# TensorE's instructions kept in source order from the third token group on, and the attention's state products put right behind its output products

## Chip, cores and metric

One Trainium2 chip, one core. The metric is device time in microseconds of one launch, less is better. The kernel before takes 876.1 us (median of three runs, 875.66 to 876.71).

## What is computed

Three layers, one behind the other, on 4 x 768 = 3072 tokens of width 8 x 48 = 384: a gated linear attention with a decaying state, a gated feed-forward layer behind an RMS norm, and a layer of 8 experts of which each token uses one.

```python
def _attn_ref(q, k, v, alpha):
    for t in range(S):
        state = alpha[:, :, t, :, None] * state + np.einsum('bhd,bhe->bhde', k[:, :, t], v[:, :, t])
        y[:, :, t] = np.einsum('bhd,bhde->bhe', q[:, :, t], state)
...
def _moe_ref(x, w_gate, w_val, w_out, rms_g):
    xn = x / np.sqrt(np.mean(x * x, axis=-1, keepdims=True) + 1e-06) * rms_g
    g = xn @ w_gate
    return g * (1.0 / (1.0 + np.exp(-g))) * (xn @ w_val) @ w_out
...
def _moe2_ref(x, w_gate, w_output_gate, w1, w2):
    e_idx = np.argmax(x @ w_gate, axis=1)
    for e in range(E):
        mask = e_idx == e
        h = np.maximum(x[mask] @ w1[e], 0.0)
        out[mask] = gate_w[mask, None] * eom[mask, e, None] * (h @ w2[e])
```

## The kernel before

The tokens are cut into 24 tiles of 128, three tiles to a group, so there are eight groups (`g` 0 to 7). Tiles 0 to 17 take turns among three of the four sequences, tiles 18 to 23 are the fourth sequence. The attention goes chunk by chunk: a chunk is one tile, and its sequential loop is replaced by products inside the tile and a state carried from tile to tile of a sequence.

**Attention, `stages(t)`.** Five stages for a tile, each a short piece of TensorE work and a closure `post` with what other engines do behind it:

- score (`ps_s`, line 416): eight products of q and k, one for each head, even heads on the lower rows of the array and odd heads on the upper ones. Behind it VectorE multiplies by the mask (`P`, line 426), and the state is decayed and copied to `wide` (lines 420, 422).
- transposes of k (`ps_k`, line 436), copied to `kn` by ScalarE.
- output (`ps_y`): four products of q with the state (line 447), sixteen of `P` with v (line 451). Behind it the RMS norm: square and sum on ScalarE, a power on GpSimd, the scaling to `xn` on ScalarE (lines 457 to 460).
- state (`ps_st`, line 472): eight products of k and v, added to the state by VectorE. The last tile of a sequence has neither this nor the transposes of k.
- transposes of `xn` (`ps_x`, line 493), copied to the feed-forward layer's input in a high and a low part, `xh` and `xl`.

Ahead of them `prework(t)` prepares q and k with scans and multiplications on VectorE. From tile 8 on it uses no TensorE.

**Feed-forward layer.** A group makes 36 slots: for each of 12 blocks of 128 hidden columns a gate product (`ps_g`), a value product (`ps_v`) and an output product (`ps_o`). Each slot is nine matmuls of 384 or 400 columns in fp32r, because every operand is split in a high and a low part (`mm3`, line 595, and `m_out`, line 629). VectorE multiplies gate and value (`tt`, line 606) and makes the low part `hl` (line 615); ScalarE makes the gate's activation and the high part `hh` (lines 587, 609). Groups 0 and 1 are cut in two runs each (`runs`), and while they run the weights arrive and are converted on VectorE and ScalarE: `F` or `Fo`, then the high part, then the low part (`wgl`, `wvl`, `wol`, line 531).

**What sets the order.** The loops call `slot` for a slot and `stage` for the next stage when it is due; `NST` (5) is the number of stages a tile counts for. That is the order of the source. The program is then put in order for each engine by a scheduler, which runs the instructions through a model of the engines and lets an engine take a later instruction when an earlier one isn't ready in the model. `tc.keep_in_program_order(ins)` takes that freedom away: instructions marked so keep the order of the source among themselves on their engine. `pace` marks a few on other engines; TensorE's products of the attention and of the feed-forward layer are not marked.

**PSUM.** The attention's tiles share three banks (pool `psA`), the feed-forward layer has five.

After the eight groups come the experts (`e_h`, `e_o`), from about 625 us to the end.

Of the kernel before, what the change touches and what calls it, by code (L numbers as in the profile page):

```python
# [42 lines left out]
    'RB': 9,  # L43
    'LEADG': 6,
    'NAT': 5,
    'PET': 8,
    'NO': 'arkq',
}
# [4 lines left out]
def gla_glu_moe_kernel(  # L53
# [16 lines left out]
    nc = tc.nc  # L70
    P = 128
    B, H, S, D = q.shape
# [3 lines left out]
    NTILE = NT // P  # L76
    KD = DM // P
# [5 lines left out]
    GT = 3  # L83
# [20 lines left out]
    ident = const.tile([P, P], F32, name="ident")  # L104
# [9 lines left out]
    tri_b = const.tile([P, P], BF16, name="tri_b")  # L114
    ones_b = const.tile([P, P], BF16, name="ones_b")
# [86 lines left out]
    vt = {}  # L202
    pre = {}
    xT = {}
    SEATS = CFG['SEATS']
    spread = [True]
    junk = [psM.tile([P, 4, P], F32, tag='o2', name='junk')]
    paced = [CFG['K0']]

# [191 lines left out]
    def stages(t):  # L401
        b, c = place_of[t]
        first, final = c == 0, c == NCH - 1
        en, qT, kT = pre[t]
        Sc = state_of[b % BS]
        S_ = wide[0]
        rs = [slice(64 * hh, 64 * hh + D) for hh in range(2)]
        g, ti = divmod(t, GT)
        Pt = {}

        def score():
            ps = [bank([P, NP, P], "ps_s") for _ in range(2)]
            for p in range(NP):
                for hh in range(2):
                    r = slice(64 * hh, 64 * hh + D)
                    nc.tensor.matmul(ps[hh][:, p, :], lhsT=kT[r, p, :], rhs=qT[r, p, :], start=True, stop=True)  # L416

            def post():
                if not first:
                    nc.vector.tensor_tensor(out=Sc, in0=Sc, in1=en.to_broadcast([P, NP, D]), op=ALU.mult)  # L420
                    for hh in range(2):
                        nc.scalar.activation(S_[rs[hh], :, hh * D:hh * D + D], Sc[rs[hh]], AF.Copy)
                mb = mask.to_broadcast([P, NP, P])
                for hh in range(2):
                    Ph = seat_of(t, f"P{hh}", [P, NP, P])
                    pace(f'Ph{t}', nc.vector.tensor_tensor(out=Ph, in0=ps[hh], in1=mb, op=ALU.mult))
                    Pt[hh] = Ph
            return post
        yield score

        def ktr():
            if final:
                return None
            ps = bank([P, NP, P], "ps_k")
            for p in range(NP):
                nc.tensor.transpose(ps[:, p, :], kT[:, p, :], ident)  # L436
            kn = seat_of(t, "kn", [P, H, 64])
            nc.scalar.activation(kn, ps.rearrange("p a (h d) -> p (a h) d", h=2), AF.Copy)
            Pt["kn"] = kn
            return None  # L440
        yield ktr

        def outp():
            ps = bank([P, DM], "ps_y")
            if not first:
                for p in range(NP):
                    nc.tensor.matmul(ps[:, p * 2 * D:p * 2 * D + 2 * D], lhsT=qT[:, p, :], rhs=S_[:, p, :],  # L447
                                     start=(p == 0), stop=False, skip_group_check=True)
            for h in (0, 2, 4, 6, 1, 3, 5, 7):
                for u in (slice(0, 64), slice(64, P)):  # L450
                    nc.tensor.matmul(ps[u, h * D:h * D + D], lhsT=Pt[h % 2][:, h // 2, u], rhs=vt[t][:, h, :],  # L451
                                     start=first, stop=True, skip_group_check=True)
# [12 lines left out]
        def state():  # L465
            if final:
                return None
            kn = Pt["kn"]
            ps = bank([P, NP, D], "ps_st")
            for p in range(NP):  # L470
                for hh in range(2):
                    nc.tensor.matmul(ps[64 * hh:64 * hh + 64, p, :], lhsT=kn[:, 2 * p + hh, :],  # L472
                                     rhs=vt[t][:, 2 * p + hh, :], start=True, stop=True)

            def post():
                if first:
                    nc.scalar.activation(Sc, ps, AF.Copy)
                else:
                    nc.vector.tensor_tensor(out=Sc, in0=ps, in1=Sc, op=ALU.add)
            return post  # L480
        yield state

        def xtr():
            if t and t + 2 < NTILE:
                load_v(t + 2)
            if ti == 0:
                xT[g] = (act.tile([P, KD, G], F32R, tag="xh", name="xh"),
                         act.tile([P, KD, G], F32R, tag="xl", name="xl"))
            xh, xl = xT[g]
            xn = Pt["xn"]  # L490
            ps = bank([P, KD, P], "ps_x")
            for kc in range(KD):
                nc.tensor.transpose(ps[:, kc, :], xn[:, kc * P:kc * P + P], ident)  # L493
# [84 lines left out]
    obank = {}  # L578
# [12 lines left out]
    def mm3(ps, wh, wl, xh, xl):  # L591
        n = 0
        for kc in range(KD):
            for a_, b_ in ((wh, xh), (wh, xl), (wl, xh)):
                nc.tensor.matmul(ps, lhsT=a_[:, kc, :], rhs=b_[:, kc, :],  # L595
                                 start=(n == 0), stop=(n == 3 * KD - 1))
                n += 1

    def m_val(g, j):
# [21 lines left out]
    def m_out(s, j):  # L621
        g, j0, j1 = runs[s]
        if j == j0:
            obank[s] = [psM.tile([P, WO], F32, tag=f"o{i}", name="ps_o") for i in range(GT)]
        hh, hl, _ = hbuf.pop((g, j))
        for i in range(GT):
            sl = slice(i * P, i * P + P)
            for n, (a_, b_) in enumerate(((hh, "woh"), (hh, "wol"), (hl, "woh"))):
                nc.tensor.matmul(obank[s][i], lhsT=a_[:, sl], rhs=weight(b_, j),  # L629
                                 start=(j == j0 and n == 0), stop=(j == j1 - 1 and n == 2))  # L630

    rows = {}

# [55 lines left out]
    def route_b(g):  # L689
        oh, ohb, ohc, m8, og, se = rt.pop(g)  # L690
        R = rows[g]
        ps = psR[0].tile([P, GT + 1, E], F32, tag=psR[1], name="ps_r")
        nc.tensor.matmul(ps[:, 0:1, :], lhsT=tri_b, rhs=ohb[:, 0:1, :], start=True, stop=True)
        for i in range(1, GT):
            nc.tensor.matmul(ps[:, i, :], lhsT=tri_b, rhs=ohb[:, i, :], start=True, stop=False)
            nc.tensor.matmul(ps[:, i, :], lhsT=ones_b, rhs=ohc[:, i - 1, :], start=False, stop=True)
        nc.tensor.matmul(ps[:, GT, :], lhsT=ones_b, rhs=ohc[:, GT - 1, :], start=True, stop=True)
        bc = [P, GT, E]

        nc.vector.tensor_scalar(out=se, in0=se, scalar1=1e-9, scalar2=2.0, op0=ALU.add, op1=ALU.mult)  # L700
# [83 lines left out]
            m_out(s - 1, runs[s - 1][2] - 1)  # L784
            return lambda: m_evac(s - 1)

    NST = 5
    LOADS = CFG['LOADS']
    for x in LOADS.split():
        if x[0] == "v":  # L790
# [41 lines left out]
    spread[0] = False  # L832
    prep.extend(prework(GT))

    att_stream = (st for t in range(GT, NTILE) for st in stages(t))
    nprep = GT + 1
    AHEAD = CFG['AHEAD']
    done = 0
    GS = GT * NST
# [385 lines left out]
    u = U - 1  # L1225
# [121 lines left out]
```

## Time and profile before

| | us |
|---|---|
| median of three runs | 876.1 |
| the profiled execution | 880.26 |
| its span, first to last instruction | 878.6 |
| TensorE busy with matmuls | 856.1 |
| TensorE's weight loads | 814.5 |
| VectorE busy | 489.3 |
| ScalarE busy | 326.0 |
| chain that ended last: share of TensorE | 85% |

A busy share counts an instruction from start to end, and TensorE's matmuls overlap each other, so that the row of busy time says little of how fast they follow. In the timeline the distance from one start to the next is what counts. There one instruction of an fp32 product shows as two records (x2), so x16 is all eight score products of a tile.

### The profile page before, as it was taken

How to read it: one execution, taken by the hardware profiler on the slowest of the kernel's cores; microseconds unless marked ns; L12 is line 12 of the kernel's file. 1: busy time of each engine (PE TensorE's matmuls, PEld its weight loads, DVE VectorE, ACT ScalarE, POOL GpSimd, SP SyncE). 2: the span in 40 equal slices, each digit the busy share in tenths (PEclk: the TensorE clock that was granted, in tenths of full speed). 3: DMA queues.
4: the chain of work that ended last, by engine and by line, in shares of the span. 5: the costliest groups of instructions: out<-in, count | busy, mean ns of one | idle time of the engine just before them, and what ended most of it. 6: DMA issues, size and time to landing. Idle time of an engine off the chain costs nothing.

```text
span 878.6 us, 15655 instructions
## 1 busy us (share of the span) xinstructions
PE 856.1 (97%) x6042; PEld 814.5 (93%) x6042; DVE 489.3 (56%) x1108; ACT 326.0 (37%) x708; POOL 143.8 (16%) x204
## 2 busy tenths in 40 slices
PE   7999999999999999999999999999999999999994
PEld 6799999899999999999999999999988999999994
DVE  7899987576854656655665552244454443444330
ACT  1655554234333233332322333334234442445431
POOL 2001001001100100010010010013032343344331
PEclk8999999999999999999999999999999999999998
DMA  9855534493311222132231010023056164256510
GB/s 190 181 163 149 175 83 122 117 258 89 104 49 36 78 57 61 43 87 60 59 87 47 13 37 1 1 93 98 1 182 197 60 212 144 65 190 198 178 41 24
DMA packets 121660, 88.46 MB, mean 101 GB/s; under 512 B 58219, under 2 KB 116716, under 8 KB 121584
## 3 DMA queue, kind: packets, MB, share of 16 engines
q1 hardware_dynamic: 117120, 77.97, 33.4%
q0 software_dynamic: 4464, 9.48, 3.1%
q8 instruction: 48, 0.79, 0.4%
q14 instruction: 28, 0.23, 0.1%
HBM read 71.62 MB, written 16.07 MB: 100 GB/s over the span
## 4 chain that ended last, share of the span: by engine, by line
PE 85%; DMA 5%; issue 4%; DVE 2%; POOL 1%; ACT 1%; SPq 1%; POOLq 0%; DVEq 0%; ACTq 0%
PE ps_o L629 18%; PE ps_v L595 18%; PE ps_g L595 18%; PE ps_b L1037 8%; PE ps_h L595 7%; PE ps_s L416 4%; PE ps_y L451 3%; DMA st<-in_moe_w_dram 3%; PE ps_y L447 2%; DMA er<-bucket 1%; PE ps_st L472 1%; PE ps_k L436 1%; PE ps_x L493 1%; POOL out_dram L1053 1%; PE pc L560 1%
## 5 line engine op out<-in xcount | busy, mean ns | idle before, releaser
L606 DVE TENSOR_TENSOR tt<-tt,ps_v 128x384 f32<-128x384 f32 x96 | 52.8, 550 | 140.9 <-PE ps_v L595 136.5
L587 ACT ACTIVATE tt<-ps_g 128x384 f32<-128x384 f32 x96 | 47.0, 490 | 135.4 <-PE ps_g L595 132.3
L609 ACT ACTIVATE hh<-tt 128x384 fp32r<-128x384 f32 x96 | 50.2, 523 | 119.6 <-DVE tt L606 119.2
L615 DVE TENSOR_TENSOR hl<-tt,hh 128x384 fp32r<-128x384 f32 x96 | 54.4, 567 | 28.1 <-ACT hh L609 27.4
L1037 PE MATMUL ps_b<-w2a,h 128*128 128x384 f32 (+2 forms) x336 | 67.4, 339 | 1.1 <-ACT h L1021 1.1
L595 PE MATMUL ps_g<-xh,wgh 128*128 128x384 f32 x192 | 68.1, 355 | 0.0
L595 PE MATMUL ps_v<-xh,wvh 128*128 128x384 f32 x192 | 68.0, 354 | 0.0
L1022 DVE SCALAR_TENSOR_TENSOR h<-ps_h,h 128x256 fp32r<-128x256 f32 (+6 forms) x72 | 38.0, 531 | 52.3 <-ACT h L1021 52.0
L629 PE MATMUL ps_o<-wol,hh 128*128 128x400 f32 x192 | 66.6, 347 | 0.0
L629 PE MATMUL ps_o<-woh,hh 128*128 128x400 f32 x192 | 66.5, 353 | 0.0
L1037 PE MATMUL ps_b<-w2b,h 128*114 128x384 f32 (+3 forms) x336 | 65.0, 338 | 0.2 <-ACT h L1021 0.2
L595 PE MATMUL ps_g<-xh,wgl 128*128 128x384 f32 x192 | 65.1, 339 | 0.0
L595 PE MATMUL ps_v<-xh,wvl 128*128 128x384 f32 x192 | 65.0, 339 | 0.0
L595 PE MATMUL ps_g<-xl,wgh 128*128 128x384 f32 x192 | 64.9, 338 | 0.0
L629 PE MATMUL ps_o<-woh,hl 128*128 128x400 f32 x192 | 64.7, 346 | 0.0
L595 PE MATMUL ps_v<-xl,wvh 128*128 128x384 f32 x192 | 64.7, 337 | 0.0
L1037 PEld LDWEIGHTS ps_b<-w2a,h 128*128 128x128 f32 (+2 forms) x336 | 57.5, 181 | 2.6 <-ACT h L1021 2.0
L1037 PEld LDWEIGHTS ps_b<-w2b,h 128*114 128x114 f32 (+3 forms) x336 | 57.5, 175 | 2.1 <-ACT h L1021 0.6
L595 PE MATMUL ps_h<-x,w1b 128*128 128x456 f32 (+3 forms) x288 | 58.5, 344 | 0.3 <-DVE h L1022 0.2
L1021 ACT ACTIVATE h<-ps_h 128x256 fp32r<-128x256 f32 (+6 forms) x72 | 33.3, 467 | 64.8 <-PE ps_h L595 60.4
L595 PE MATMUL ps_h<-x,w1a 128*128 128x256 f32 (+3 forms) x288 | 53.5, 328 | 0.6 <-DVE h L1022 0.6
L458 POOL TENSOR_SCALAR ss<-ss 128x1 f32<-128x1 f32 x24 | 6.4, 266 | 281.0 <-ACT xn L457 276.1
(284 smaller groups left out, 1994.9 us busy)
## 6 DMA issues: line engine op xcount, KB each, us to landing
st<-in_moe_w_dram SPq DMA_DIRECT2D x64, 384.0 KB, 5.4
bucket<-zero SPq DMA_DIRECT2D x8, 772.0 KB, 6.2
stg<-in_moe_w_gate_dram SPq DMA_DIRECT2D x12, 384.0 KB, 3.9
stg<-in_moe_w_val_dram SPq DMA_DIRECT2D x12, 384.0 KB, 3.7
stg<-in_moe_w_out_dram SPq DMA_DIRECT2D x12, 384.0 KB, 3.0
v<-in_v_dram SPq DMA_DIRECT2D x23, 192.0 KB, 2.8
blk_a<-in_alpha_dram SPq DMA_DIRECT2D x32, 96.0 KB, 2.2
blk_k<-in_k_dram SPq DMA_DIRECT2D x32, 96.0 KB, 2.3
```

The lines of the kernel that those rows point to most:

```text
L416: nc.tensor.matmul(ps[hh][:, p, :], lhsT=kT[r, p, :], rhs=qT[r, p, :], start=True, stop=True)
L447: nc.tensor.matmul(ps[:, p * 2 * D:p * 2 * D + 2 * D], lhsT=qT[:, p, :], rhs=S_[:, p, :], start=(p == 0), stop=False, skip_group_check=True)
L451: nc.tensor.matmul(ps[u, h * D:h * D + D], lhsT=Pt[h % 2][:, h // 2, u], rhs=vt[t][:, h, :], start=first, stop=True, skip_group_check=True)
L587: nc.scalar.activation(tt, ps, AF.Silu)
L595: nc.tensor.matmul(ps, lhsT=a_[:, kc, :], rhs=b_[:, kc, :], start=(n == 0), stop=(n == 3 * KD - 1))
L606: nc.vector.tensor_tensor(out=tt, in0=tt, in1=ps, op=ALU.mult)
L609: nc.scalar.activation(hh, tt, AF.Copy)
L615: nc.vector.tensor_tensor(out=hl, in0=tt, in1=f(hh), op=ALU.subtract)
L629: nc.tensor.matmul(obank[s][i], lhsT=a_[:, sl], rhs=weight(b_, j), start=(j == j0 and n == 0), stop=(j == j1 - 1 and n == 2))
L1021: nc.scalar.activation(hh[:, 0, :], ps, AF.Relu)
L1022: nc.vector.scalar_tensor_tensor(out=hh[:, 1, :], in0=ps, scalar=0.0, in1=f(hh[:, 0, :]), op0=ALU.max, op1=ALU.subtract)
L1037: ins = nc.tensor.matmul(ob2[u][i][0:r], lhsT=hh[:, a_, sl], rhs=we[p][b_][:, j, :], start=(j == 0 and m == 0), stop=(j == KF2 - 1 and m = ...
```

## The change

Two things, both in the order of work; no product is added or left out.

- `seq` marks TensorE's products of the attention, the feed-forward layer and the routing to keep their source order. It is on in groups 2 to 6, off in groups 0 and 1 and in the last.
- `four` joins output and state to one stage, for tiles 3 to 23. `NST` is 4, so a tile's stages come three slots apart instead of 2.4. `XO` makes a stage due one slot earlier in the runs of groups 0 and 1 behind the first.

```diff
+    'XO': 1,
+    'STRICT': 4,
...
+    strict = [False]
+
+    def seq(ins):
+
+        if strict[0]:
+            tc.keep_in_program_order(ins)
...
-                    nc.tensor.matmul(ps[hh][:, p, :], lhsT=kT[r, p, :], rhs=qT[r, p, :], start=True, stop=True)
+                    seq(nc.tensor.matmul(ps[hh][:, p, :], lhsT=kT[r, p, :], rhs=qT[r, p, :], start=True, stop=True))
...
-    NST = 5
+    NST = 4
...
+    def four(t):
+
+        s_, k_, y_, d_, x_ = stages(t)
+
+        def yd():
+            posts = [y_(), d_()]
+
+            def post():
+                for p in posts:
+                    if p:
+                        p()
+            return post
+        return s_, k_, yd, x_
+
+    att_stream = (st for t in range(GT, NTILE) for st in four(t))
...
-        return (n + 1 + N * (s - 2)) * GS >= (k_ + 1) * 2 * N and k_ < GS and (k_ < NST - 1 or s >= CFG['XG'])
+        return (n + 1 + CFG['XO'] + N * (s - 2)) * GS >= (k_ + 1) * 2 * N and k_ < GS and (k_ < NST - 1 or s >= CFG['XG'])
...
+        strict[0] = s >= CFG['STRICT']
...
+        strict[0] = g + 2 >= CFG['STRICT'] and not last
```

The same `seq(...)` stands around the products of `ktr`, `outp`, `state`, `xtr`, `mm3`, `m_out` and `route_b`.

On TensorE in the third group, from the end of one tile (`ps_x`) over the next tile of the attention, before (each line "..." stands for a slot or more of the feed-forward layer, nine matmuls each):

```order
L493 MATMUL ps_x<-ident,xn 128x128 x3
...
L416 MATMUL ps_s<-qT,kT 128x128
...
L416 MATMUL ps_s<-qT,kT 128x128 x7
...
L436 MATMUL ps_k<-ident,kT 128x128 x4
...
L447 MATMUL ps_y<-wide_125,qT 128x96
...
L447 MATMUL ps_y<-wide_125,qT 128x96
...
L447 MATMUL ps_y<-wide_125,qT 128x96 x2
L451 MATMUL ps_y<-v,P_3041 64x48 x8
L451 MATMUL ps_y<-v,P_3043 64x48 x8
...
L472 MATMUL ps_st<-v,kn 64x48 x8
```

And the same tile in the changed kernel:

```order
L502 MATMUL ps_x<-ident,xn 128x128 x3
...
L425 MATMUL ps_s<-qT,kT 128x128 x8
...
L445 MATMUL ps_k<-ident,kT 128x128 x4
...
L456 MATMUL ps_y<-wide_125,qT 128x96 x4
L460 MATMUL ps_y<-v,P_3041 64x48 x8
L460 MATMUL ps_y<-v,P_3043 64x48 x8
L481 MATMUL ps_st<-v,kn 64x48 x8
```

Eight pieces between slots became four, with three slots between any two of them: the score is whole, the output is whole, and the state products follow it.

On VectorE in the first group, where nothing is marked by `seq` but the scheduler's order follows TensorE's, before (`aT`, `qT`, `kT` are the preparation of an attention tile, `stg`, `F`, `Fo` a weight block):

```order
L531 TENSOR_TENSOR wgl_198<-F_654,wgh_197 128x3x128
L420 TENSOR_TENSOR state1_123<-state1_123,en_576 128x192
L315 SCALAR_TENSOR_TENSOR qT_556<-ps_n_571,begin_127 128x512
L340 TENSOR_TENSOR kT_557<-ps_n_656,aT_555 128x512
L515 TENSOR_SCALAR Fo_744<-stg_173 128x384
L531 TENSOR_TENSOR wvl_316<-F_697,wvh_315 128x3x128
L304 MEMSET begin_127 128x3
L606 TENSOR_TENSOR tt_715<-tt_715,ps_v_726 128x384
```

And the same place in the changed kernel:

```order
L429 TENSOR_TENSOR state1_123<-state1_123,en_596 128x192
L540 TENSOR_TENSOR wgl_198<-F_631,wgh_197 128x3x128
L615 TENSOR_TENSOR tt_694<-tt_694,ps_v_711 128x384
L324 SCALAR_TENSOR_TENSOR qT_576<-ps_n_591,begin_127 128x512
L540 TENSOR_TENSOR wvl_316<-F_685,wvh_315 128x3x128
L524 TENSOR_SCALAR Fo_729<-stg_173 128x384
L540 TENSOR_TENSOR wol_517<-Fo_589,woh_516 128x400
```

The multiplication `tt`, which needs the value product from TensorE, now stands ahead of a scan and of a weight block's low part, and the multiplication of `kT` has gone further back.

## Rows read from the trace of the kernel before

**Rows 1.** Span and mean granted TensorE clock of the core.

```profile
core 0: 878.6 us, clock 0.990
```

**Rows 2.** Busy time in two stretches; columns: stretch, sum, PE, PEld, DVE, ACT, POOL, PEclk, DMA.

```profile
40.00:100.00 60.00, 59.42 (x498) 56.70 (x498) 57.21 (x133) 34.94 (x83) 3.51 (x7) 1.00 0.56 158
195.00:555.00 360.00, 360.00 (x2733) 340.99 (x2732) 203.40 (x484) 116.83 (x279) 32.59 (x63) 1.00 0.22 56
```

**Rows 3.** TensorE's timeline: nine matmuls of one slot, first and ninth; columns: start, us.

```profile
249.05 0.34 PE L595 MATMUL ps_v<-xh,wvh 128*128 128x384 f32 x1
...
250.44 0.34 PE L595 MATMUL ps_v<-xh,wvl 128*128 128x384 f32 x1
```

**Rows 4.** TensorE's timeline: the score products of one tile, cut in one and seven.

```profile
242.18 0.34 PE L595 MATMUL ps_g<-xh,wgl 128*128 128x384 f32 x1
242.45 0.48 PE L416 MATMUL ps_s<-qT,kT 48*128 48x128 f32 x2
242.86 0.44 PE L595 MATMUL ps_v<-xh,wvh 128*128 128x384 f32 x1
243.14 0.34 PE L595 MATMUL ps_v<-xl,wvh 128*128 128x384 f32 x1
...
246.30 1.16 PE L416 MATMUL ps_s<-qT,kT 48*128 48x128 f32 x14
247.38 0.45 PE L595 MATMUL ps_g<-xh,wgh 128*128 128x384 f32 x1
```

**Rows 5.** TensorE's timeline: a tile whose eight score products stand together.

```profile
222.94 1.16 PE L416 MATMUL ps_s<-qT,kT 48*128 48x128 f32 x16
224.04 0.18 PE L693 MATMUL ps_r<-ohb,tri_b 128*128 128x8 bf16 x1
```

**Rows 6.** TensorE's timeline: output and state products of one tile, cut.

```profile
252.51 0.34 PE L629 MATMUL ps_o<-woh,hl 128*128 128x400 f32 x1
252.69 0.36 PE L447 MATMUL ps_y<-wide,qT 128*128 128x96 f32 x2
...
253.09 0.34 PE L595 MATMUL ps_g<-xl,wghe 128*128 128x384 f32 x1
...
256.28 0.58 PE L447 MATMUL ps_y<-wide,qT 128*128 128x96 f32 x4
256.79 1.14 PE L451 MATMUL ps_y<-v,P 128*64 128x48 f32 x32
257.86 0.45 PE L629 MATMUL ps_o<-woh,hh 128*128 128x400 f32 x1
...
261.00 0.34 PE L595 MATMUL ps_g<-xh,wgle 128*128 128x384 f32 x1
261.27 0.67 PE L472 MATMUL ps_st<-v,kn 128*64 128x48 f32 x16
261.87 0.44 PE L595 MATMUL ps_v<-xh,wvhe 128*128 128x384 f32 x1
262.15 0.34 PE L595 MATMUL ps_v<-xl,wvhe 128*128 128x384 f32 x1
```

**Rows 7.** TensorE's timeline: output and state products that stand together in an early tile.

```profile
145.54 1.14 PE L451 MATMUL ps_y<-v,P 128*64 128x48 f32 x32
146.50 0.64 PE L472 MATMUL ps_st<-v,kn 128*64 128x48 f32 x16
147.07 0.44 PE L595 MATMUL ps_v<-xh,wvhe 128*128 128x384 f32 x1
```

**Rows 8.** VectorE's and ScalarE's timelines: mask and norm of the same tile.

```profile
247.28 1.29 DVE L426 TENSOR_TENSOR P<-ps_s,mask 128x512 f32<-128x512 f32 x2 [0.77 <-PE ps_s L416]
...
259.59 0.58 ACT L460 ACTIVATE xn<-ps_y,ss 128x384 f32<-128x384 f32 x1 [0.94 <-POOL ss L459]
```

**Rows 9.** VectorE's costliest groups; columns: busy us, mean ns, idle before.

```profile
L315 DVE TENSOR_TENSOR_SCAN aT<-aT,begin 128x512 f32<-128x512 f32 x19 | 23.1, 1217 | 0.1
L340 DVE TENSOR_TENSOR kT<-ps_n,aT 128x512 f32<-128x512 f32 x3 | 2.0, 670 | 0.0
```

More of the change, by code (lines that the diff above doesn't have):

```diff
@@ L435, in ktr @@
             for p in range(NP):
-                nc.tensor.transpose(ps[:, p, :], kT[:, p, :], ident)
+                seq(nc.tensor.transpose(ps[:, p, :], kT[:, p, :], ident))
             kn = seat_of(t, "kn", [P, H, 64])
@@ L446, in outp @@
                 for p in range(NP):
-                    nc.tensor.matmul(ps[:, p * 2 * D:p * 2 * D + 2 * D], lhsT=qT[:, p, :], rhs=S_[:, p, :],
-                                     start=(p == 0), stop=False, skip_group_check=True)
+                    seq(nc.tensor.matmul(ps[:, p * 2 * D:p * 2 * D + 2 * D], lhsT=qT[:, p, :], rhs=S_[:, p, :],
+                                     start=(p == 0), stop=False, skip_group_check=True))
             for h in (0, 2, 4, 6, 1, 3, 5, 7):
                 for u in (slice(0, 64), slice(64, P)):
-                    nc.tensor.matmul(ps[u, h * D:h * D + D], lhsT=Pt[h % 2][:, h // 2, u], rhs=vt[t][:, h, :],
-                                     start=first, stop=True, skip_group_check=True)
+                    seq(nc.tensor.matmul(ps[u, h * D:h * D + D], lhsT=Pt[h % 2][:, h // 2, u], rhs=vt[t][:, h, :],
+                                     start=first, stop=True, skip_group_check=True))
             def post():
@@ L471, in state @@
                 for hh in range(2):
-                    nc.tensor.matmul(ps[64 * hh:64 * hh + 64, p, :], lhsT=kn[:, 2 * p + hh, :],
-                                     rhs=vt[t][:, 2 * p + hh, :], start=True, stop=True)
+                    seq(nc.tensor.matmul(ps[64 * hh:64 * hh + 64, p, :], lhsT=kn[:, 2 * p + hh, :],
+                                     rhs=vt[t][:, 2 * p + hh, :], start=True, stop=True))
             def post():
@@ L492, in xtr @@
             for kc in range(KD):
-                nc.tensor.transpose(ps[:, kc, :], xn[:, kc * P:kc * P + P], ident)
+                seq(nc.tensor.transpose(ps[:, kc, :], xn[:, kc * P:kc * P + P], ident))
             sl = slice(ti * P, ti * P + P)
@@ L594, in mm3 @@
             for a_, b_ in ((wh, xh), (wh, xl), (wl, xh)):
-                nc.tensor.matmul(ps, lhsT=a_[:, kc, :], rhs=b_[:, kc, :],
-                                 start=(n == 0), stop=(n == 3 * KD - 1))
+                seq(nc.tensor.matmul(ps, lhsT=a_[:, kc, :], rhs=b_[:, kc, :],
+                                 start=(n == 0), stop=(n == 3 * KD - 1)))
                 n += 1
@@ L628, in m_out @@
             for n, (a_, b_) in enumerate(((hh, "woh"), (hh, "wol"), (hl, "woh"))):
-                nc.tensor.matmul(obank[s][i], lhsT=a_[:, sl], rhs=weight(b_, j),
-                                 start=(j == j0 and n == 0), stop=(j == j1 - 1 and n == 2))
+                seq(nc.tensor.matmul(obank[s][i], lhsT=a_[:, sl], rhs=weight(b_, j),
+                                 start=(j == j0 and n == 0), stop=(j == j1 - 1 and n == 2)))
     rows = {}
@@ L692, in route_b @@
         ps = psR[0].tile([P, GT + 1, E], F32, tag=psR[1], name="ps_r")
-        nc.tensor.matmul(ps[:, 0:1, :], lhsT=tri_b, rhs=ohb[:, 0:1, :], start=True, stop=True)
+        seq(nc.tensor.matmul(ps[:, 0:1, :], lhsT=tri_b, rhs=ohb[:, 0:1, :], start=True, stop=True))
         for i in range(1, GT):
-            nc.tensor.matmul(ps[:, i, :], lhsT=tri_b, rhs=ohb[:, i, :], start=True, stop=False)
-            nc.tensor.matmul(ps[:, i, :], lhsT=ones_b, rhs=ohc[:, i - 1, :], start=False, stop=True)
-        nc.tensor.matmul(ps[:, GT, :], lhsT=ones_b, rhs=ohc[:, GT - 1, :], start=True, stop=True)
+            seq(nc.tensor.matmul(ps[:, i, :], lhsT=tri_b, rhs=ohb[:, i, :], start=True, stop=False))
+            seq(nc.tensor.matmul(ps[:, i, :], lhsT=ones_b, rhs=ohc[:, i - 1, :], start=False, stop=True))
+        seq(nc.tensor.matmul(ps[:, GT, :], lhsT=ones_b, rhs=ohc[:, GT - 1, :], start=True, stop=True))
         bc = [P, GT, E]
@@ L833, in gla_glu_moe_kernel @@
     prep.extend(prework(GT))
-    att_stream = (st for t in range(GT, NTILE) for st in stages(t))
+    def four(t):
[9 more added lines that the diff above has]
+    att_stream = (st for t in range(GT, NTILE) for st in four(t))
     nprep = GT + 1
```

## Prediction

> **What bounds the kernel now.** I read the clock first, then the busy time by stretch, then TensorE's timeline, start by start. The granted clock is 0.990 over the span [rows 1] and 1.00 in both stretches that matter here [rows 2], so no term below hangs on it. From 195 to 555 us, where the change pins TensorE's order, TensorE is busy 360.00 of 360 us while VectorE has 203.40 and ScalarE 116.83 [rows 2]: TensorE sets the pace, and nothing else is near its limit. From 40 to 100 us it is otherwise: VectorE has 57.21 of 60 us [rows 2], since it converts weights there, and whatever TensorE saves there is worth little.
>
> That TensorE is "busy" all the time says nothing of how well. Matmuls overlap, so the distance between starts is the price. Inside a slot it is (250.44 - 249.05) / 8 = 0.174 us [rows 3]. At a piece of the attention it is more: a piece costs its own products and an edge on either side. With the single score product of rows 4 the two neighbours are 243.14 - 242.18 = 0.96 us apart where two strides would be 0.35, so this one product costs 0.61 us. Its seven sisters need, from their start to the next instruction's, 247.38 - 246.30 = 1.08 us [rows 4]. All eight together need 224.04 - 222.94 = 1.10 us [rows 5]. So the eighth product is nearly free when it stands with the others, and costs 0.6 us when it stands alone. That is what the change can win.
>
> **The change, part by part.** How often a piece is cut is counted in TensorE's order of the two programs, from the third group's start to the last tile; 15 tiles' score products lie there.
>
> *Score products whole.* Before, nine tiles are cut in 1 and 7, three in 2 and 6, one in 1, 1 and 6, and two are whole. In the changed order all 15 are whole. A cut in 1 and 7 costs 0.61 + 1.08 - 1.10 = 0.59 us, times nine is 5.3. For 2 and 6 there is no row here; two heads on different halves of the array should cost about what one does (0.61), and six should take a quarter less than eight, so that about 0.4 is left: 1.2 for three. This lies between nothing and the 0.59 of the other cut. The threefold cut costs 0.61 + 0.4 = 1.0. Sum: 7.5 us.
>
> *State behind output.* Alone, the state products put their neighbours 262.15 - 261.00 = 1.15 us apart, 0.80 more than two strides [rows 6]. In the early tile where they follow the output products directly they take 147.07 - 146.50 = 0.57 us, and the output products 146.50 - 145.54 = 0.96 [rows 7] instead of 257.86 - 256.79 = 1.07 [rows 6]. So joining saves 0.80 - 0.57 + 0.11 = 0.34 us. Eleven tiles have state products there: 3.7 us.
>
> *The four products with the state (`wide`).* Before they are often cut too, but one alone costs 253.09 - 252.51 - 0.35 = 0.23 us, and two inside a piece cost 256.79 - 256.28 = 0.51 [rows 6], 0.25 each. Making these whole saves nothing, and I count nothing.
>
> *Two small items.* Tile 18 has two single `P` products cut off its output; between the 0.23 of rows 6 and the 0.61 of rows 4 I take 0.4 each, 0.8 in all. Against that, the routing products stood twice right behind a score or state piece before and always stand alone after; an edge of 0.1 us each, 0.2 lost.
>
> Pinned stretch: 7.5 + 3.7 + 0.8 - 0.2 = 11.8 us less. All of it is on the path, as TensorE is busy throughout.
>
> *What a pinned piece waits for.* TensorE now stays in front of a piece whose operand is late, with the whole feed-forward layer behind it; before, the scheduler put slots ahead of it. So the slack decides. The masked scores are ready at 247.28 + 1.29 = 248.57 us [rows 8] and used at 256.79 [rows 6], 8.2 us later; in the new order six slots (54 x 0.174 = 9.4 us) stand between score and output, so that slack stays. `xn` is scaled by 259.59 + 0.58 = 260.17 us [rows 8], 2.3 us after the output products ended at about 257.86; in the new order three slots (4.7 us) and the state products stand between, about 3 us of slack. `kn` has three slots, where it needs one copy. The preparation of the next tile is VectorE's, with 157 us free in the stretch. The output and state pieces take two of the three PSUM banks at once; what was in them is the score, evacuated by the mask six slots before. On SP's queue the load of v moves ahead of some pieces of q; its user is two tiles (24 slots, some 38 us) away, so I count nothing, and if it blocked the queue, q would have a tile's time to spare. What is hidden here is hidden by the slots between the pieces; without them every one of these waits would be TensorE's.
>
> *The early groups.* Nothing is pinned in groups 0 and 1, but the stages come three slots apart, output and state are joined, and the scheduler gives a new order. VectorE's work is the same, and it is full. At the place shown in the part on the change, a `tt`, which needs TensorE's value product, moved ahead of a scan (1217 ns) and of a multiplication of `kT` (670 ns) [rows 9]. If VectorE has to wait there for what it used to fill with these, 1.9 us are lost; two such places would make 3.8. The other end is a gain: VectorE is idle for 60 - 57.21 = 2.8 us [rows 2], and if a better order closed all of that, 2.8 us would be won. I take one wait of 1.9 less some 0.6 of the possible gain: 1.3 us lost. It is nearer the loss, as a full engine can't make up for a wait.
>
> *After the last tile* no product moves. The experts start earlier by what is gained and keep their own length.
>
> **Sum.** -11.8 + 1.3 = -10.5 us. The profiled execution took 880.26 us with a span of 878.6; it would go to 869.8 and 868.1. The median of the runs is 876.1, 4.2 us under the profiled execution. **876.1 - 10.5 = 865.6 us.**
>
> **Rivals.** About 0.2% (1.8 us) is what a measurement of this kernel can tell from no change.
>
> *TensorE has no room, and nothing comes of it* (876.1 us). For it: TensorE's busy time fills its whole stretch [rows 2]. Against it: the distances between starts in rows 4 to 7. The Trainium skill, "Perfetto Trace Analysis", section "Identifying the Most-Contended Engine", calls the busy share of matmuls a bad measure of the room that is left, because pipelined instructions mislead, and names the busy share of weight loads instead. By the busy row the sum would be 0; by that rule the room is 360 - 340.99 = 19.0 us, and the 11.8 fit in it. This trace agrees with the rule. Chance 0.04.
>
> *Whole score pieces are dearer than rows 5 shows.* The whole piece is seen there with routing products behind it, which may hide part of its end; if a whole piece cost as much as its two parts did, only the joined state and the small items would be left, 4.3 - 1.3 = 3.0 us less: 873.1. Against it: the seven alone already take 1.08. With a part of it, or an early loss at its upper end, the result lies between 868 and 873. Chance 0.14.
>
> *The norm comes late, and TensorE waits at every tile* (slower). The place is the transposes of `xn` behind output and state. The chain square, power, scaling goes through ScalarE, GpSimd and ScalarE, and ScalarE's queue also holds the feed-forward layer's activations, each of which waits for TensorE or VectorE in turn; if the scaling stands behind one that waits for the next slot, `xn` is a slot or two late. The slack is 3 us. Fifteen tiles times 0.7 us of waiting would eat the 10.5; so it decides from a delay of 3.7 us behind today's. At a wait of 1.4 us a tile the time would be 865.6 + 21 = 886.6. For it: pinned pieces can't be passed. Against it: ScalarE is busy a third of the time, and today's chain takes 2.3 us with ScalarE's other work in it. Chance 0.07.
>
> **From this to the numbers.** My forecast, 861.5 to 868 (876.1 - 11.8 - 2.8 at one end, 876.1 - 11.8 + 3.8 at the other), has 0.75; the dearer pieces 0.14, no effect 0.04, the late norm 0.07. The range goes from 862.5, where the early gain is not quite whole, to 872.5, which takes in most of the second rival. Faster by over 0.2%: 0.75 + 0.14 = 0.89; the same: 0.04; slower: 0.07.
>
> **What would show it.** In the timeline of the changed kernel, from about 200 to 545 us: every score piece as one x16 of about 1.1 us; x32 of the output followed by x16 of the state with 0.96 and 0.57 us between starts; four pieces a tile; TensorE waiting for nothing there. In 40 to 100 us a wait of TensorE for a weight part or a wait of VectorE for `ps_v`, 1 to 2 us in all. The first matmul of the experts some 10 us earlier, and the same distance kept to the end. I am wrong if the waits list TensorE in front of `ps_x`, `ps_y` or `ps_s` in the pinned stretch for more than a microsecond in all, or if whole pieces are longer than 1.3 us, or if the early stretch moves by more than 4 us.

## The result and the profile after

| | before | after |
|---|---|---|
| median of four runs, us | 876.4 (875.66 to 878.18) | 868.35 (867.92 to 869.86) |
| the profiled execution, us | 880.26 | 869.86 |
| its span, us | 878.6 | 868.2 |

The four runs of before are the three shown ahead and one beside the change. The ratio is 0.9903, interval [0.9882, 0.9925]: faster by 1%, some 8 us, where the forecast said 10.5 us and 865.6. The time lies in the stated range, 2.75 us above the forecast, and 0.35 above the 861.5 to 868 that the forecast's own bounds gave.

First the clock and the busy time by stretch in the kernel after, as in [rows 1, 2]; columns: stretch, sum, PE, PEld, DVE, ACT, POOL, PEclk, DMA.

```profile
core 0: 868.2 us, clock 0.990
40.00:100.00 60.00, 57.71 (x485) 54.74 (x484) 54.93 (x126) 32.06 (x80) 4.34 (x7) 0.97 0.54 154
200.00:545.00 345.00, 344.57 (x2700) 333.87 (x2699) 203.73 (x482) 116.69 (x277) 39.45 (x61) 1.00 0.23 59
```

The pinned stretch reads like before: TensorE busy all the time at a clock of 1.00, the others far from full. Its busy share has not moved and yet the stretch is shorter. The early stretch has changed: TensorE has lost 1.7 us of its 59.42 and the clock is 0.97.

Now the two kinds of pieces in TensorE's timeline after; a whole score, then output and state of the same tile, each with its neighbours (columns: start, us).

```profile
246.97 0.34 PE L638 MATMUL ps_o<-woh,hl 128*128 128x400 f32 x1
247.24 1.16 PE L425 MATMUL ps_s<-qT,kT 48*128 48x128 f32 x16
248.33 0.45 PE L604 MATMUL ps_g<-xh,wgh 128*128 128x384 f32 x1
...
258.42 1.03 PE L456 MATMUL ps_y<-wide,qT 128*128 128x96 f32 x8
259.38 1.14 PE L460 MATMUL ps_y<-v,P 128*64 128x48 f32 x32
260.35 0.64 PE L481 MATMUL ps_st<-v,kn 128*64 128x48 f32 x16
260.91 0.44 PE L604 MATMUL ps_g<-xh,wghe 128*128 128x384 f32 x1
```

The whole score needs 248.33 - 247.24 = 1.09 us, also in front of an ordinary slot; [rows 5] had 1.10 in front of routing products, [rows 4] 1.08 for seven of the eight. The output products take 0.97 and the state behind them 0.56 ([rows 6, 7]: 0.96 and 0.57 forecast).

To see where the time went I set three marks in each timeline: the first gate product (**A**), the first of the tenth block of hidden columns (**B**, where most of the early conversion is over), and the experts' first product (**C**). Up to each mark the same slots have run in all kernels, to within three matmuls. Before:

```profile
38.77 0.44 PE L595 MATMUL ps_g<-xh,wgh 128*128 128x384 f32 x1
...
106.37 0.34 PE L595 MATMUL ps_g<-xh,wgh 128*128 128x384 f32 x1
...
625.55 0.40 PE L595 MATMUL ps_h<-x2a,w1a 128*128 128x256 f32 x2
```

and after:

```profile
36.98 0.45 PE L604 MATMUL ps_g<-xh,wgh 128*128 128x384 f32 x1
...
107.03 0.34 PE L604 MATMUL ps_g<-xh,wgh 128*128 128x384 f32 x1
...
615.50 0.40 PE L604 MATMUL ps_h<-x2a,w1a 128*128 128x256 f32 x2
```

From A to B it was 67.60 us and is 70.05: 2.45 lost. From B to C it was 519.18 and is 508.47: 10.71 won. From C to the end it was 253.05 and is 252.70, as forecast. Mark A itself is 1.79 us earlier, in a stretch that the change does not reorder. Over all traces A goes with the granted clock up to it: 0.87 in the four with A at 38.7 to 38.8 us (before is one of them), 0.95 here, 1.00 in the nine with A at 35.5 to 36.2. One kernel stands at both ends (`again` 38.71, `change_beside` 36.22), so it is the clock of an execution and not the change. Net of it the change wins 8.26 us up to the experts, which is what the medians show (8.05).

B to C can be split once more, at the 31st block (the seventh of the third group; up to it the attention's pieces are the same in both kernels too, to within a few small products). Before:

```profile
240.69 0.42 PE L595 MATMUL ps_g<-xh,wgh 128*128 128x384 f32 x1
```

and after:

```profile
242.25 0.42 PE L604 MATMUL ps_g<-xh,wgh 128*128 128x384 f32 x1
```

From B to this mark it was 134.32 us and is 135.22: 0.90 lost. From the mark to C it was 384.86 and is 373.25: 11.61 won.

**The early loss.** TensorE's timeline after, from the last output slot ahead of tile 5's `xn` pieces:

```profile
85.55 0.35 PE L638 MATMUL ps_o<-woh,hl 128*128 128x400 f32 x1
86.90 0.55 PE L502 MATMUL ps_x<-ident,xn 128*128 128x128 f32 x3 [1.00 <-ACT xn L469]
87.28 0.74 PE L569 MATMUL pc<-wr,wT 128*128 128x16 f32 x6
87.87 0.52 PE L561 MATMUL pt<-ident,Fo 128*128 128x128 f32 x3
88.98 0.84 PE L569 MATMUL pc<-wr,wT 128*128 128x16 f32 x6 [0.58 <-ACT wT L563]
89.67 0.43 PE L604 MATMUL ps_g<-xh,wgh 128*128 128x384 f32 x1
...
91.00 0.52 PE L604 MATMUL ps_g<-xl,wgh 128*128 128x384 f32 x1
91.32 0.52 PE L604 MATMUL ps_g<-xh,wgl 128*128 128x384 f32 x1
```

The same place before, and GpSimd's power behind that tile's sum, after and before:

```profile
87.66 0.34 PE L629 MATMUL ps_o<-woh,hl 128*128 128x400 f32 x1
87.84 0.49 PE L493 MATMUL ps_x<-ident,xn 128*128 128x128 f32 x3
```

```profile
84.73 1.50 POOL L468 TENSOR_TENSOR ss<-ss,mhalf 128x1 f32<-128x1 f32 x1
```

```profile
85.45 0.55 POOL L459 TENSOR_TENSOR ss<-ss,mhalf 128x1 f32<-128x1 f32 x1
```

Two things happen in the early stretch. In the new order nine output matmuls stand between the tile's state products and its `xn` pieces where seven value and nine output matmuls stood, and the power took 1.50 us instead of 0.55: TensorE waits 1.00 us for `xn`. While the power ran, VectorE had two instructions behind one another that read two operands from SBUF each, and the power ended 0.43 us behind the second:

```profile
84.78 0.55 DVE L530 SCALAR_TENSOR_TENSOR Fo<-stg,Fo 128x384 int32<-128x384 int32 x1
85.24 0.56 DVE L540 TENSOR_TENSOR wvl<-F,wvh 128x384 fp32r<-128x384 f32 x1
```

At four later tiles of the change the power takes 1.40 to 1.55 us too, each time with a scan of 1.2 us on VectorE beside it; there the slack hides it. This is an overlap that the trace shows and no run tests, and at other tiles the power stays at 0.55 although such an instruction starts 0.05 us behind it.

And behind this wait and the small pieces that follow, the matmuls are 0.32 us apart instead of 0.174: the granted clock fell. The stretches 85 to 90 and 90 to 93.6 us after, columns as in [rows 2]:

```profile
85.00:90.00 5.00, 3.42 (x25) 2.85 (x25) 2.91 (x7) 3.10 (x10) 1.23 (x1) 1.00 0.96 270
90.00:93.60 3.60, 3.60 (x14) 3.58 (x13) 3.60 (x10) 0.78 (x3) 0.00 (x0) 0.53 0.01 5
```

0.53 is about the lower of the two levels (1.2 GHz).

### The profile page after: what moved, and what is told of

It reads as the page before. It is cut to its first block, busy times and chain, and to the rows that moved or that the text cites. A ratio compares the mean times of both kernels' runs of the same rounds, so it can differ in the third digit from the quotient of the medians.

```text
span 868.2 us, 15665 instructions
## 1 busy us (share of the span) xinstructions
PE 843.2 (97%) x6042; PEld 810.5 (93%) x6042; DVE 488.8 (56%) x1108; ACT 325.9 (38%) x708; POOL 152.2 (18%) x204
## 4 chain that ended last, share of the span: by engine, by line
PE 77%; DMA 6%; DVE 6%; issue 5%; ACT 2%; POOL 2%; SPq 1%; POOLq 0%; DVEq 0%; ACTq 0%
PE ps_g L604 17%; PE ps_o L638 17%; PE ps_v L604 17%; PE ps_b L1061 8%; PE ps_h L604 7%; DMA st<-in_moe_w_dram 4%; PE ps_s L425 3%; PE ps_y L460 2%; PE ps_y L456 2%; PE ps_k L445 1%; PE ps_st L481 1%; PE ps_x L502 1%; POOL out_dram L1077 1%; DMA blk_a<-in_alpha_dram 1%; PE ps_t L1025 1%
## 5 line engine op out<-in xcount | busy, mean ns | idle before, releaser
L604 PE MATMUL ps_v<-xh,wvh 128*128 128x384 f32 x192 | 66.0, 344 | 0.0
L467 POOL TENSOR_SCALAR ss<-ss 128x1 f32<-128x1 f32 x24 | 10.8, 448 | 301.0 <-ACT xn L466 298.2
```

The lines of the kernel that those rows point to most:

```text
L604: seq(nc.tensor.matmul(ps, lhsT=a_[:, kc, :], rhs=b_[:, kc, :], start=(n == 0), stop=(n == 3 * KD - 1)))
```

## The experiments

| kernel | ratio, interval | A to B | B to C |
|---|---|---|---|
| `again` (the change) | 0.9907 [0.9878, 0.9936] | +0.86 | -10.70 |
| `change_beside` (the change) | 0.991 [0.9893, 0.9927] | +2.42 | -10.43 |
| `pin_five` | 0.9937 [0.9913, 0.9961] | +0.41 | -6.33 |
| `join_only` | 0.997 [0.9956, 0.9984] | +2.47 | -4.21 |
| `late_join` | 0.9909 [0.988, 0.9937] | -0.02 | -9.80 |
| `halves` | 1.0012 [0.9993, 1.003] | +3.99 | -2.44 |
| `x_next_slot` | 1.0064 [1.0041, 1.0086] | +2.40 | +3.89 |
| `pin_all` | 0.9931 [0.9906, 0.9956] | +4.85 | -7.96 |
| `due_old` | 0.9925 [0.9902, 0.9947] | +3.88 | -10.46 |
| `mixed_run3` | 0.9863 [0.9835, 0.9892] | +0.01 | -12.70 |
| `mixed_beside` (the same) | 0.9867 [0.9844, 0.9891] | 0.00 | -12.70 |
| `mixed_due` | 0.9846 [0.9822, 0.9871] | 0.00 | -13.90 |

Ratios are to the kernel before, run beside each. The last two columns are us, worked out from the marks of each trace as above. The medians scatter by 2 to 3 us; B to C repeats within 0.3 us (first two rows, and the two runs of one kernel further down), so the marks tell more. In every kernel of the table that has the pins and the joined stages, save `halves` and `x_next_slot`, the stretch from the 31st block to C wins 11.4 to 11.6 us: what tells them apart lies ahead of it.

**The change again.**

> The changed kernel again, in five rounds, so that the other runs have it on their chip. Theory A (the early loss is in the order): about 8 us faster than before again, and in a second profile TensorE waits about 1 us for xn at tile 5's transposes near 86 us and the granted clock then falls to 1.2 GHz for some 3.6 us, as in the first profile. Theory B (the early loss was chance of one execution, a power on GpSimd of 1.50 us instead of 0.55): no such wait, no fall of the clock, and the first nine-block mark (the tenth gate product) comes no later than 106.5 us from a first gate product at the same distance.

870.67 us. B to C repeats. TensorE waits 1.0 us for `xn` at tile 5 again, but the clock is 1.00 there, and the early loss is 0.86 instead of 2.45: the fall of the clock costs 1.6 us and does not always come. (From the rows above: eight matmuls at 0.32 instead of 0.174 are 1.2 us, and the piece ahead of them makes most of the rest.) Nor is it always as long: in `due_old` and `halves` the clock is 0.54 over some 7 us, and the early loss 3.9. The power takes 1.50 us in all seven traces with this order of the early tiles, so that is not chance.

**The pins alone**, five stages and the old due times.

```diff
-    'XO': 1,
+    'XO': 0,
...
-    NST = 4
+    NST = 5
...
-    att_stream = (st for t in range(GT, NTILE) for st in four(t))
+    att_stream = (st for t in range(GT, NTILE) for st in stages(t))
```

> Pins alone: TensorE's order kept from group 2 on, but five stages as before, output and state apart, no earlier stage in groups 0 and 1. Theory A (whole score pieces are worth 0.6 us each, joined state products 0.34, and the early groups lose by their new order): the early groups take what they took before, score pieces are whole, state pieces cost 0.80 as before; 6 to 8 us less than before, 868.5 to 870.5. Theory C (the pins do nothing by themselves, the gain is that of the joined stage and its wider spacing): no change, 875.5 to 877.

872.48 us, 2 us above what Theory A gave. B to C wins 6.33. At the third group's start something stands in the timeline that the kernel before doesn't have:

```profile
198.72 0.49 PE L502 MATMUL ps_x<-ident,xn 128*128 128x128 f32 x3
200.80 0.44 PE L604 MATMUL ps_g<-xh,wgh 128*128 128x384 f32 x1 [1.59 <-ACT xh L509]
201.39 0.44 PE L604 MATMUL ps_g<-xl,wgh 128*128 128x384 f32 x1 [0.16 <-DVE xl L510]
201.67 0.34 PE L604 MATMUL ps_g<-xh,wgl 128*128 128x384 f32 x1
```

The starts are 2.08, 0.59 and 0.28 us apart; without waiting they would be 0.25, 0.17 and 0.17, so this place costs 2.36, about what the time missed by. Without it the pins alone win 8.7, where my terms for them (7.5 + 0.8 - 0.2) make 8.1.

**The joining alone**, nothing pinned.

```diff
-    'STRICT': 4,
+    'STRICT': 99,
```

> Joined stages alone: four stages as in the change, but no TensorE instruction pinned. The scheduler still cuts score pieces (12 of 1 or 2, and 6 or 7 behind them, from group 2 on) but puts the state products behind the output. Theory A: joined state 3.7 us less, early loss 1.3 to 2.5 us; together 1 to 4 us less than before, 872.5 to 875.5. Theory C: the whole gain, 867 to 869.5.

875.66 us. B to C wins 4.21; my term for the joined state was 3.7. Pins alone and joining alone add up to 10.54, and the change wins 10.43 to 10.71, but that they agree is luck: the pins alone lose 2.36 at the third group's start where the change loses 0.98. Behind the 31st block, where the pins alone wait for nothing, they win 8.65 up to C and the joining alone 4.59, 13.2 together, where the change wins 11.61: some 1.6 us are in both. The joining alone also cuts the scores otherwise, in 2 and 6 at seven tiles where it was three, in 1 and 7 at five where it was nine. Most of the scores are still cut here, and the early loss is all there, with a clock of 0.80 in 90 to 94 us.

**The joining only from tile 9 on.**

```diff
-    'XO': 1,
+    'XO': 0,
...
-    NST = 4
+    NST = 5
...
-    att_stream = (st for t in range(GT, NTILE) for st in four(t))
+    att_stream = (st for t in range(GT, NTILE) for st in (stages(t) if t < 3 * GT else four(t)))
...
+    NST, done = 4, 2 * GT * 4
     for g in range(2, NG):
```

> Groups 0 and 1 as before (five stages, tiles 3 to 8), joined stages and pins from group 2 on. Theory A: the early groups keep their time of before, so this is 1.3 to 2.5 us faster than the change: 865.5 to 867.5. Theory B (early loss was chance): the same as the change within 0.7 us.

869.54 us: 1.1 under the change beside it, and 2 us above what Theory A gave, so the median decides for neither. The marks do: from A to B nothing is lost (-0.02), and B to C keeps 9.80 of the gain, with the wait of 1.59 for `xh` in it. So the early loss comes with what the change does to the stages of the early tiles, the joining, the four stages or the due time.

**Eight score products half by half.**

```diff
-            for p in range(NP):
-                for hh in range(2):
+            for p, hh in ([(p, hh) for hh in range(2) for p in range(NP)] if t >= 3 * GT else
+                          [(p, hh) for p in range(NP) for hh in range(2)]):
```

> The change, but from tile 9 on the eight score products come half by half: the four even heads (lower rows of the array), then the four odd heads (upper rows), where the change alternates. Same products, same length, same place. If the eighth product is nearly free because it runs beside one on the other half of the array (my reading of the rows), neighbours on the same half cannot overlap, and a whole score piece costs up to 0.9 us more: from 1.29 to about 2.2 us, 15 tiles make 13 us, time 882. If the 0.6 us of a lone product are an edge (entering and leaving a piece) that is paid once per piece whatever is in it, the order inside the piece does not matter: 1.29 us, time as the change within 2 us.

880.18 us. The score piece in TensorE's timeline:

```profile
248.13 0.34 PE L638 MATMUL ps_o<-woh,hl 128*128 128x400 f32 x1
248.39 1.71 PE L425 MATMUL ps_s<-qT,kT 48*128 48x128 f32 x16
250.03 0.44 PE L604 MATMUL ps_g<-xh,wgh 128*128 128x384 f32 x1
```

1.64 us instead of 1.09, the same eight products: 0.55 more, and 15 of them make 8.25. B to C is 8.3 worse than in the change. So the order of heads inside a piece matters, but by 0.55 and not by 0.9, and the rival (a piece has an edge that is paid once) holds a part. What makes the order matter is not settled: even and odd heads lie on different halves of the array, as in my reading, but they also write different PSUM banks (`ps[hh]`), and this run changes both alternations at once.

**The `xn` pieces one slot behind output and state.** A condition is added to the stage's due time; nothing else.

```diff
-            if done < (NTILE - GT) * NST and ((g - 1) * 3 * KF + n + 1 + CFG['LEADG']) * GT >= (done + 1 - GT * NST) * 3 * KF / NST:
+            if done < (NTILE - GT) * NST and ((g - 1) * 3 * KF + n + 1 + CFG['LEADG']) * GT >= (done + 1 - GT * NST) * 3 * KF / NST or (done % NST == 3 and 3 * GT * NST <= done + GT * NST):
```

> The change, but the transposes of xn come one slot behind output and state instead of three, in groups 1 to 6. This takes away the slack that the prediction gave the norm (about 3 us): one slot of 1.6 us and the state products of 0.6 stand against a chain square, power, scaling of 2.3 us behind the output products. If the slack was as the prediction worked it out, TensorE now waits in front of ps_x at most tiles for some 0.1 to 1 us each, 1 to 15 us in all, and where nothing is pinned less. If the chain is shorter than read, no waits show and the time is the change's; if ScalarE's queue delays it (the rival of the late norm), the waits are 2 us or more a tile and the time is over 890.

884.63 us. TensorE's waits for `xn` in this kernel (total, times, longest; one of the 15 is tile 5's), and one of them in the timeline:

```profile
PE ps_x L502 <- ACT xn L469: 12.2, 15, 1.4
```

```profile
262.67 0.34 PE L604 MATMUL ps_g<-xh,wgle 128*128 128x384 f32 x1
263.67 0.55 PE L502 MATMUL ps_x<-ident,xn 128*128 128x128 f32 x3 [0.66 <-ACT xn L469]
263.98 0.42 PE L604 MATMUL ps_v<-xh,wvhe 128*128 128x384 f32 x1
```

Slower than the kernel before: B to C is 14.6 us worse than in the change. This is the late norm of the rivals, made to happen: it needs one slot instead of three. A wait that the profile shows as 0.66 costs 0.88, since the start before it is 1.00 away instead of 0.18 and the one behind 0.31 instead of 0.25.

**Everything pinned**, groups 0 and 1 too.

```diff
-    'STRICT': 4,
+    'STRICT': 0,
```

> The change, with TensorE's order pinned in groups 0 and 1 too, where VectorE is full with converting weights. If a pinned piece or slot cannot be passed while its weight part is late (my reading of why the change leaves these groups free), TensorE waits there for ps_g, ps_v or ps_o behind weight parts for 4 us or more in all, the mark of the third group's start moves 3 to 13 us later than in the change, and the time is 873 to 883. If the early loss comes from the scheduler's own order and not from VectorE, pinning the source's order does no harm: the marks stay within 1.5 us of the change and the time at 868 to 870.

874.08 us. The early loss is 4.85 instead of 2.42, and B to C is worse by 2.5 to 2.7 too. Two of its waits that the change doesn't have:

```profile
PE pt L561 <- DVE Fo L530: 2.9, 1, 2.9
PE ps_v L604 <- DVE tt L615: 1.1, 1, 1.1
```

The first is a wait for a weight's first form (`Fo`), at its transposes and not in a slot as I had expected, the second one for VectorE's `tt`. The time lies where I put it. The loss goes on behind B: from A up to the 31st block this kernel falls 5 us behind the change, and from there it wins the same 11.6. Whatever whole pieces win in the early tiles is less than the waits. Where VectorE is full, the scheduler's freedom is worth something.

**The old due time.**

```diff
-    'XO': 1,
+    'XO': 0,
```

> The change with the old due time in groups 0 and 1 (XO 0): output and state joined and four stages from tile 3 on as in the change, but a stage is not due one slot earlier. It moves products from the second half of the first group on. If the earlier due time puts the transposes of xn at tile 5 too close behind the output, the 1 us wait for xn and the small pieces around it vanish, and the mark of the tenth block, from the kernel's own start, falls from 1 to 2.5 us late to within 0.6 us of the kernel before; time 866 to 868. If joining and four stages are enough for the early loss, the mark stays 0.8 us or more late and the time is the change's.

871.92 us. The 1.0 us wait for `xn` at tile 5 and the fall of the clock stay, so the due time is not their cause; with `late_join` that leaves the joining and the four stages of the early tiles. The wait of 1.59 us for `xh` at the third group's start is back, as in `pin_five`, and yet B to C is -10.46, as good as in the change. For the earlier due time costs the change elsewhere what it saves there. In the second half of the second group, which is not pinned, TensorE waits in the change for `hl` and `tt`, and in `due_old` it doesn't:

```profile
187.83 0.34 PE L638 MATMUL ps_o<-wole,hh 128*128 128x400 f32 x1
188.39 0.45 PE L638 MATMUL ps_o<-wohe,hl 128*128 128x400 f32 x1 [0.22 <-DVE hl L624]
...
191.55 0.36 PE L456 MATMUL ps_y<-wide,qT 128*128 128x96 f32 x2
192.26 0.44 PE L604 MATMUL ps_v<-xh,wvhe 128*128 128x384 f32 x1 [0.35 <-DVE tt L615]
```

The starts are 0.56 and 0.71 us apart instead of 0.18 and 0.14: 0.95 us lost (0.56 and 1.26 in the two other executions of the change).

**A version that beats both:** `late_join` with the pins from the second half of the second group.

```diff
-    'STRICT': 4,
+    'STRICT': 3,
```

> The kernel of late_join (five stages and the old due times for tiles 0 to 8, output and state joined from tile 9), with TensorE's order pinned one run earlier: from the second half of the second group instead of the third group's start. If the early stretch loses only where VectorE is full, and pinned pieces are no dearer than in the later groups, the tile that lies in that run gets its whole score for 0.6 us and nothing waits: the stage mark of the last block in front of the experts moves from -13.0 to -13.6 to -16 us against the kernel before, time 866 to 869 where late_join had 869.5. If VectorE's weight parts are still late there (theory: pinning harms wherever weights are converted), TensorE waits for weight parts (ps_g or ps_v behind wgl or wvl) for 2 us or more and the mark falls back to -11 or less.

865.49 us. The mark expected at -13.6 to -16 stands at -12.66: I had counted it from the timeline's zero, and the -13.0 of `late_join` held its own early start. From A to C it goes from -9.82 to -12.69, so the pins of this half group win 2.9 us, inside the 0.6 to 3 that the marks stood for: the scores of two tiles are cut in eight pieces in `late_join` and whole here. Once more beside the change on one chip:

> The kernel of mixed_run3 once more, beside the change on the same chip. If its lead comes from the early groups (old stages there) and from one more pinned tile, its last mark in front of the experts, taken from its own start, is again 1.5 to 4 us ahead of the change's, and its time 863 to 868. If the lead was the scatter of one chip, the two agree within 1 us.

> The change as it is, beside mixed_beside. Pinned stretch: its marks win 10.5 to 11.1 us again between the tenth and the ninety-fourth block, and the time is 866 to 871. In the early groups TensorE waits about 1 us for xn at tile 5; whether the granted clock falls to the lower level behind it (once in two executions so far) is open.

865.6 us against 870.33. The intervals do not overlap, nothing is lost from A to B, and B to C wins 2.3 more than the change beside it, 12.70 both times; the change's 10.43 lies just under what was expected. From A to C the lead is 4.7, a little more than expected. It still waits 1.59 us for `xh`, so the last run takes the earlier due time for that half group alone, which is pinned now:

```diff
-    'XO': 0,
+    'XO': 1,
...
-        return (n + 1 + CFG['XO'] + N * (s - 2)) * GS >= (k_ + 1) * 2 * N and k_ < GS and (k_ < NST - 1 or s >= CFG['XG'])
+        return (n + 1 + (CFG['XO'] if s == 3 else 0) + N * (s - 2)) * GS >= (k_ + 1) * 2 * N and k_ < GS and (k_ < NST - 1 or s >= CFG['XG'])
```

> The kernel of mixed_run3, with the change's earlier due time in the second half of the second group alone: the last tile's xn pieces of that group come one slot earlier there. Four kernels with the old due time (pin_five, late_join, mixed_run3, due_old) wait 1.6 us for xh at the third group's first gate product, the change and pin_all with the new one 0.2. If the due time is what sets this wait, it falls from 1.6 to about 0.2 us here, the experts' first product comes 14.0 to 14.4 us earlier than in the kernel before (from its own start; 12.7 in mixed_run3), and the time is 863 to 866. If the wait came from the five stages of the early tiles, or the earlier products are cut up or wait elsewhere, it stays above 1 us or the gain shows up as another wait, and the mark stays at 12.4 to 13.2.

```profile
PE ps_g L604 <- ACT xh L509: 0.2, 1, 0.2
```

863.54 us. The wait is gone, no wait for `tt` or `hl` has come in its place, and the mark is 13.9 us earlier, 0.1 short of what was expected: here the earlier due time wins 1.2. The intervals of this kernel and of `mixed_run3` overlap; the marks tell them apart.

## Why the prediction was right, and where it was off

*What bounds the kernel.* Right. TensorE is as busy as before, and 10.7 us came out of its "full" stretch. The Trainium skill, "Perfetto Trace Analysis", section "Identifying the Most-Contended Engine", judges TensorE's room by the weight loads' share (and by the share of its peak rate), not by that of the matmuls; by the weight loads there were 19.0 us of room in 360 [rows 2], 5.3%, and now there are 345 - 333.87 = 11.1, 3.2%. The trace agrees.

*Score pieces whole* (7.5). Right in size. By the rows after, a cut in 1 and 7 costs 0.61 + 1.08 - 1.09 = 0.60, forecast 0.59. `pin_five` without its wait gives 8.7 for all that the pins do, forecast 8.1. The change wins 11.61 behind the 31st block, where 11.4 of the forecast 11.8 lie.

*Why a lone product is dear.* Half right. I said the eighth product is nearly free with the others. `halves` shows that 0.55 us of the piece hang on the alternation of even and odd heads; whether on that of the array's halves or of the PSUM banks is open. What is left belongs to the piece as a whole. I had not kept the two apart, and the sum did not need it.

*State behind output* (3.7). Right: 0.97 and 0.56 between starts, against 1.07 and 0.80 alone [rows 6], are the 0.34 a tile. The 4.2 of `join_only` does not show the term by itself, since it holds a part of the scores too.

*What a pinned piece waits for.* This step missed a place. I went through score, output, state, `kn` and `xn`, which wait for nothing in the later groups, and did not ask about the first gate product of a group, which needs the `xh` and `xl` of the tile just finished. In the change it reads so:

```profile
202.63 0.34 PE L638 MATMUL ps_o<-wohe,hl 128*128 128x400 f32 x1
203.19 0.44 PE L604 MATMUL ps_g<-xh,wgh 128*128 128x384 f32 x1 [0.22 <-ACT xh L509]
203.85 0.44 PE L604 MATMUL ps_g<-xl,wgh 128*128 128x384 f32 x1 [0.21 <-DVE xl L510]
204.13 0.34 PE L604 MATMUL ps_g<-xh,wgl 128*128 128x384 f32 x1
```

Starts 0.56, 0.66 and 0.28 apart instead of 0.18, 0.17 and 0.17: 0.98 us lost. Before, the scheduler put a value product between the two gate products there.

*The slack of `xn`.* Nearly right. I had about 3 us, as the chain takes 2.3. In the change ScalarE ends the scaling 3.0 us behind the end of the output (the state's start), not 2.3, and `xn` is used 2.4 us later. Of the 0.7 more, 0.6 is GpSimd's first small instruction behind the square, 0.78 us instead of 0.19, again with a scan on VectorE beside it:

```profile
262.80 0.58 ACT L469 ACTIVATE xn<-ps_y,ss 128x384 f32<-128x384 f32 x1 [1.53 <-POOL ss L468]
```

```profile
265.78 0.49 PE L502 MATMUL ps_x<-ident,xn 128*128 128x128 f32 x3
```

So the rival of the late norm needed 2.4 us more, and `x_next_slot` shows what it would have cost (14.6 us; my 21 was for 1.4 us at each of 15 tiles, where 0.8 are listed on the mean).

*The early groups* (+1.3). The mis-sized term: +2.45, +0.86 and +2.42 in three executions, inside the bounds of -2.8 to +3.8, and that is luck, as the mechanism was another one. I expected VectorE to wait for `ps_v`; what came is TensorE's wait for `xn` at tile 5 and, in two of the three, the fall of the clock behind it. It was the rival of the late norm at one tile, in a place where I had counted no slack. And I had written that no term hangs on the clock; this one does.

*Sum.* -10.71 + 2.45 is -8.26 where I had -11.8 + 1.3 = -10.5. Of the 2.2 between them 1.1 is the early stretch and 1.1 lies between B and C, all of it ahead of the 31st block, where the waits of 0.98 at the third group's start and 0.95 in the half group ahead of it had no term in my sum. That the time lies in the range hangs on its upper end, which I had set for dearer pieces; the pieces are not dearer.

*The rivals.* No room: out, by B to C. Dearer whole pieces: out, 1.09 us. The late norm: not at every tile, once at tile 5.

What stays open: whether it is VectorE's two instructions that hold up GpSimd's power at tile 5, which of the two alternations makes a whole score piece cheap, and what decides whether the clock falls and for how long.

## To carry to other kernels

When an order is pinned, list every operand that comes from the stage just before, the first product of the next group too, and count the slots between; a pin is worth what its pieces save only where those slots are there. Pin where the engine is the bound, and leave the scheduler free where another engine is full. In a full engine look at the distance of starts: pieces that stand together, and whose order alternates as it does here between even and odd heads, are cheaper than the same products scattered.

## What the runs showed of the hardware

- The granted clock fell to about half (0.53, the 1.2 GHz level, over 3.6 us) behind a wait of 1.00 us and 2.8 us of transposes and 16-column products, among them a wait of 0.58. Of the seven traces with that wait, six show a clock under 1 in 90 to 94 us (0.50 to 0.80) and one 1.00; none of the other seven is under 1 there (the kernel before, with the same small pieces and no 1.00 us wait, has 1.00 [rows 2]).
- Eight score products of 48 rows take 1.09 us when they alternate between the two halves of the array, and with them between two PSUM banks, and 1.64 one half, and bank, after the other.
- A wait of TensorE costs more than the profile lists: 0.66 us listed cost 0.88, and 0.22 and 0.21 cost 0.98 together, since the starts of the matmuls behind a wait are further apart as well.
- GpSimd's power on 128x1 took 0.55 us at most tiles and 1.40 to 1.55 at five of the change's 24, each of them beside a VectorE scan or two VectorE instructions with two operands in SBUF.
